# Linear attention into a gated feed-forward block: two quotients moved a group later, two chain operands in PSUM, the last first product moved ahead, low parts of the weights over 14 steps

## The chip, the cores and the metric

The kernel runs on one core of one Trainium2 chip. The metric is the device time of one execution in microseconds. The kernel before was timed three times, with a median of 1181.67 us. One more execution was taken by the hardware profiler; its own time and its span (first to last instruction) are in the table below.

Engines are named as the profile names them: PE (matrix products), PEld (its weight loads), DVE (VectorE), ACT (ScalarE), POOL (GpSimd), SP (the engine that issues most DMAs).

## The reference, cut to what matters

```
def _attn_ref(q, k, v, w_phi):                      # q, k, v: 8 x 8 x 576 x 64, w_phi: 64 x 128
    def phi(x):
        proj = einsum('bhsd,df->bhsf', x, w_phi)
        proj = proj - max(abs(proj), axis=-1)
        return concatenate([exp(proj), exp(-proj)], axis=-1)
    q_p, k_p = phi(q), phi(k)
    kv = einsum('bhsf,bhsd->bhfd', k_p, v)
    z = sum(k_p, axis=2)
    num = einsum('bhsf,bhfd->bhsd', q_p, kv)
    den = einsum('bhsf,bhf->bhs', q_p, z)[..., None] + 1e-06
    return num / den

def _moe_ref(x, w_in, w_out):                       # x: 4608 x 512, w_in: 512 x 2048, w_out: 2048 x 512
    h = x @ w_in
    g = h - tanh(h)
    return g @ w_out
```

The attention output, laid out as 4608 rows of 512, is the x of the second function. The weights w_in and w_out arrive as float64.

## The kernel before, in words

The work has two stages.

**First stage (attention).** A unit is one pair of heads of one batch entry; there are 32 units, and `period(i)` (line 399) runs five units at once, each one phase behind the next. The order of this stage is written out by hand (`tc.manual_schedule()`). A unit ends with a division. `denom_copy` puts the denominators in a tile `dd`, `den_recip_load` (line 346) brings them with a DMA into a narrow tile `dn`, `den_recip` (line 352) adds 1e-6 and inverts on DVE (`rn`, lines 357 and 358), sends the result to memory (`rr`) and back, broadcast, with two DMAs (`rb`, line 362). `den_mul` (line 365) multiplies numerator `d` by `rb` on POOL (line 367), and `x_store` writes the quotient to the array `xs`. The calls for the last units stand after the loop, at lines 490 to 496, outside the hand-written order.

**Second stage (feed-forward).** Tokens go in 12 groups of 384, the hidden width in 16 slices of 128, so there are 192 steps (g, f). `stage1` makes one slice of h: 12 products of 128 x 384 into the PSUM tile `ph` (line 516; three buffers), because each factor is split into a high part and a low part and three of the four cross products are kept, over four blocks of 128. Then comes a chain that forms h - tanh(h): ACT makes y = h squared (L523), `s1` (L525), `s2` (L527), `th` = tanh (L529) and a mask `mk` (L531; one buffer), and DVE makes five instructions of them:

```
            nc.vector.scalar_tensor_tensor(s1, s1, PC1, y, ALU.add, ALU.mult)        # L532
            nc.vector.scalar_tensor_tensor(s2, s2, PC2, s1, ALU.add, ALU.mult)       # L533
            nc.vector.scalar_tensor_tensor(gs, s2, PA, h, ALU.mult, ALU.mult)        # L535, gs = s2
            nc.vector.tensor_tensor(th, h, th, ALU.subtract)                         # L536
            nc.vector.copy_predicated(gs, mk.bitcast(U32), th)                       # L537
```

y, s1, s2, th and mk are in SBUF (two buffers each, `mk` one), h is in PSUM. `split_g` splits the result: ACT casts it to the high part `gh` (L543), POOL subtracts to get the low part `gl` (L544). `stage2` adds this slice's contribution to the three output tiles `po` of the group: six products of 128 x 512 with `gh` (L550, L551), then three with `gl` (L553). After 16 slices `store` copies the three tiles out of PSUM (ACT the second, DVE the other two) and writes them.

`stage1` of a step is followed by `stage2` of two steps before, so PE alternates between the two, and the chain has the time between to run. The split of the weights themselves (`split_w`, line 83) into `whi`/`who` and `wli`/`wlo` is done in the first stage for slices 0 to 6; slices 7 to 15 (18 tiles) are split in the first group's steps, by a rule on the step number at line 590: the cast of a `w_in` tile on ACT (L90), of a `w_out` tile on DVE (L92), and the low part of either on POOL (L96). The first group also splits the x of the second group (`x_split`: ACT L114, DVE L115).

Here no order is written by hand: a scheduler orders each engine's instructions, except that those wrapped in `pin` (casts, splits, low parts) keep their place in the program. Every engine runs its own instructions strictly in the order in which they stand; a buffer that is reused makes its writer wait for the last reader.

Of the kernel before, what the change touches and what calls it, by code (L numbers as in the profile page):

```python
# [8 lines left out]
F32 = mybir.dt.float32  # L9
F32R = mybir.dt.float32r  # L10
U32 = mybir.dt.uint32
# [8 lines left out]
P = 128  # L20
# [12 lines left out]
def tile_linear_attention_moe(  # L33
# [22 lines left out]
    G = 3  # L56
# [64 lines left out]
    with ExitStack() as c1:  # L121
# [230 lines left out]
        def den_recip(u, pin=lambda ins: ins):  # L352
            dn = u.dn
            rr = dr.tile([2, S], F32, tag="rr", name=f"rr{u.i}")
            w = 2 * S // P
            rn = tail.tile([P, w], F32, tag="rn", name=f"rn{u.i}")
            pin(nc.vector.tensor_scalar_add(rn, dn, 1e-6))
            nc.vector.reciprocal(rn, rn)
            nc.sync.dma_start(rr.rearrange("a s -> (a s)").rearrange("(p c) -> p c", c=w), rn)
            rb = tail.tile([P, S], F32, tag="rb", name=f"rb{u.i}", bufs=2)  # L360
            for e in range(2):
                nc.sync.dma_start(rb[e * D : (e + 1) * D, :], rr[e : e + 1, :].broadcast_to([D, S]))
            u.rb = rb

        def den_mul(u, pin=lambda ins: ins):
            x = u.rb
            pin(nc.gpsimd.tensor_tensor(x, u.d, x, ALU.mult))
# [123 lines left out]
        den_mul(units[-3])  # L491
        x_store(units[-3])
        den_recip_load(units[-1])
        den_recip(units[-2])
        den_mul(units[-2])
        x_store(units[-2])

    with ExitStack() as c2:  # L500
        xp.append(c2.enter_context(tc.tile_pool(name="xp", bufs=1, reuse_waits="tile")))
        wp.append(c2.enter_context(tc.tile_pool(name="wp", bufs=1, reuse_waits="tile")))
        gp = c2.enter_context(tc.tile_pool(name="gp", bufs=2, reuse_waits="tile"))
        gm = c2.enter_context(tc.tile_pool(name="gm", bufs=3, reuse_waits="tile"))
        ps_h = c2.enter_context(tc.tile_pool(name="ps_h", bufs=3, reuse_waits="tile", space=PSUM))
        ps_o = c2.enter_context(tc.tile_pool(name="ps_o", bufs=5, reuse_waits="tile", space=PSUM))

        def stage1(g, f, xh, xl):
            n = G
            N = n * P  # L510
            ph = ps_h.tile([P, 512], F32, tag="h", name=f"ph{g}_{f}")
            h = ph[:, 0:N]
            i = 0
            for c in range(NCT):
                for wt, x in ((wi[f][0], xh), (wi[f][0], xl), (wi[f][1], xh)):
                    nc.tensor.matmul(h, wt[:, c * P : (c + 1) * P], x[:, c, 0:N], start=(i == 0), stop=(i == 3 * NCT - 1))  # L516
                    i += 1

            def tmp(tag, dt=F32, pool=gp, **kw):
                return pool.tile([P, G * P], dt, tag=tag, name=f"{tag}{g}_{f}", **kw)[:, 0:N]  # L520

            y = tmp("y")
            nc.scalar.activation(y, h, AF.Square)  # L523
            s1 = tmp("s1")
            nc.scalar.activation(s1, y, AF.Square, bias=bias_t[:, 0:1])  # L525
            s2 = tmp("s2")
            nc.scalar.activation(s2, y, AF.Square, bias=bias_t[:, 1:2])  # L527
            th = tmp("th")
            nc.scalar.activation(th, h, AF.Tanh)  # L529
            mk = tmp("mk", bufs=1)  # L530
            nc.scalar.activation(mk, y, AF.Relu, bias=bias_t[:, 2:3])  # L531
            nc.vector.scalar_tensor_tensor(s1, s1, PC1, y, ALU.add, ALU.mult)  # L532
            nc.vector.scalar_tensor_tensor(s2, s2, PC2, s1, ALU.add, ALU.mult)  # L533
            gs = s2
            nc.vector.scalar_tensor_tensor(gs, s2, PA, h, ALU.mult, ALU.mult)  # L535
            nc.vector.tensor_tensor(th, h, th, ALU.subtract)  # L536
            nc.vector.copy_predicated(gs, mk.bitcast(U32), th)  # L537
            return gs

        def split_g(g, f, gs, n):  # L540
            gh = gm.tile([P, G * P], F32R, tag="gh", name=f"gh{g}_{f}")[:, 0 : n * P]
            gl = gm.tile([P, G * P], F32R, tag="gl", name=f"gl{g}_{f}")[:, 0 : n * P]
            pin(nc.scalar.copy(gh, gs))  # L543
            pin(nc.gpsimd.tensor_tensor(gl, gs, f32(gh), ALU.subtract))  # L544
            return gh, gl

        def stage2(po, f, gh, gl, n):
            for t in range(n):
                a = gh[:, t * P : (t + 1) * P]
                nc.tensor.matmul(po[t], a, wo[f][0], start=(f == 0), stop=False)  # L550
                nc.tensor.matmul(po[t], a, wo[f][1], start=False, stop=False)  # L551
            for t in range(n):
                nc.tensor.matmul(po[t], gl[:, t * P : (t + 1) * P], wo[f][0], start=False, stop=(f == NF - 1))  # L553

        def store(t, po, n):
            for i in range(n):
                o = gp.tile([P, DM], F32, tag="o", name=f"o{t + i}", bufs=3)
                if i == 1:
                    nc.scalar.copy(o, po[i])
                else:  # L560
                    nc.vector.tensor_copy(o, po[i])
                nc.sync.dma_start(out[(t + i) * P : (t + i + 1) * P, :], o)

        NG = NT // G
        steps = [(g, f) for g in range(NG) for f in range(NF)]
        late = list(range(2 * AHEAD, 2 * NF))
        NL = len(late)
        po, gs, gg = {}, {}, {}
        for i in range(len(steps) + 2):
            if i < len(steps):  # L570
                g, f = steps[i]
                if f == 0:
                    po[g] = [ps_o.tile([P, DM], F32, tag="o", name=f"po{g}_{t}") for t in range(G)]
                gs[i] = stage1(g, f, *xt[g][:2])
                if g + 1 < NG:
                    if f == 0:
                        xt[g + 1] = x_tiles(g + 1)
                    if f % 3 == 0 and f < 3 * NCT:
                        x_load(g + 1, xt[g + 1], f // 3)
                    if f % 3 == 2 and f < 3 * NCT:  # L580
                        x_split(xt[g + 1], f // 3, pin)
            if 1 <= i <= len(steps):
                g, f = steps[i - 1]
                gg[i - 1] = split_g(g, f, gs.pop(i - 1), G)
            if i == 1:
                den_recip(units[-1], pin)
            if i == 2:
                den_mul(units[-1], pin)
                x_store(units[-1])
            while late and late[0] <= 2 * AHEAD + i * NL // (NF - 1):  # L590
                split_w(late.pop(0), pin)()
            if i >= 2:
                g, f = steps[i - 2]
                stage2(po[g], f, *gg.pop(i - 2), G)
                if f == NF - 1:
                    store(g * G, po.pop(g), G)
# [55 lines left out]
```

## Time and profile before

| | |
|---|---|
| median of 3 runs (lowest, highest) | 1181.67 us (1179.06, 1183.47) |
| the profiled execution: time, span | 1179.44 us, 1177.6 us |
| granted PE clock, mean over the span | 0.998 |
| busy share of PE, PEld, DVE, ACT, POOL | 98%, 81%, 77%, 68%, 35% |
| first product of the second stage | 356.01 us |
| longest groups of the chain that ended last | PE ph L516 33%, PE po L553, L550 and L551 11% each |

PE is busy nearly all the time, so what another engine does shows in the time only where PE has to wait for it. Such places are read from the list of PE's waits and from the timeline; in the timeline a row gives the start, the duration, the engine, the line, the instruction, the tiles as output<-input, and in brackets the idle time of the engine before the row with what ended it.

### The profile page before, as it was taken

The page shows a single profiled execution, that of the slowest core. Times are in us where ns is not written, and L with a number is a line of the kernel's source. Part 1 is how long each engine was busy: PE and PEld are TensorE (multiplying, and loading weights), DVE is VectorE, ACT ScalarE, POOL GpSimd, SP SyncE. Part 2 cuts the span into 40 slices and gives each one's busy share as a digit, 9 for nine tenths or more (in the row PEclk, how much of TensorE's full clock was granted, in tenths as well). Part 3 has the DMA queues.
Part 4 walks back from the last instruction along what each step waited for, and adds up shares of the span by engine and source line. Part 5 has one row for each costly group of instructions (what it writes and reads, how often), then busy time and mean ns, then how long its engine had stood idle before and what let it go on. Part 6 is the DMA issues. An engine that isn't in the chain of part 4 may idle for free.

```text
span 1177.6 us, 21218 instructions
## 1 busy us (share of the span) xinstructions
PE 1157.2 (98%) x7840; PEld 950.1 (81%) x7840; DVE 907.6 (77%) x1464; ACT 806.0 (68%) x1748; POOL 412.6 (35%) x404
## 2 busy tenths in 40 slices
PE   8999999999998999999999999999999999999998
PEld 6666666666656889999999999999999999999996
DVE  6999998989877977777777767777777767777665
ACT  4777776666666767676676667676666767666665
POOL 2566664455435652222222222222222222222222
PEclk9999999999999999999999999999999999999999
DMA  5565565566551000010000001000000001000000
GB/s 165 178 194 190 180 206 183 189 189 209 182 177 61 14 19 30 14 41 15 34 14 34 21 8 41 14 34 21 34 14 35 15 13 41 14 28 1 28 1 28
DMA packets 51177, 85.64 MB, mean 73 GB/s; under 512 B 13312, under 2 KB 28160, under 8 KB 51072
## 3 DMA queue, kind: packets, MB, share of 16 engines
q1 hardware_dynamic: 50912, 84.20, 22.2%
q8 instruction: 62, 1.02, 0.3%
q14 instruction: 43, 0.35, 0.1%
q10 hardware_dynamic: 160, 0.07, 0.0%
HBM read 65.08 MB, written 19.02 MB: 71 GB/s over the span
## 4 chain that ended last, share of the span: by engine, by line
PE 91%; DVE 3%; POOL 2%; DMA 2%; ACT 1%; issue 1%; DVEq 0%; SPq 0%; POOLq 0%; ACTq 0%
PE ph L516 33%; PE po L553 11%; PE po L550 11%; PE po L551 11%; PE pp L214 7%; PE pc L267 6%; PE po L314 5%; PE ptt L236 3%; PE pd L329 3%; PE pk L285 2%; PE ptk L301 1%; DMA rb<-rr 1%; PE ptr L242 1%; DMA dn<-dd 1%; DVE s L537 0%
## 5 line engine op out<-in xcount | busy, mean ns | idle before, releaser
L544 POOL TENSOR_TENSOR gl<-s,gh 128x384 fp32r<-128x384 f32 x192 | 197.9, 1031 | 569.1 <-ACT gh L543 562.8
L516 PE MATMUL ph<-xh,wli 128*128 128x384 f32 x768 | 261.0, 340 | 1.3 <-POOL wli L96 1.3
L516 PE MATMUL ph<-xl,whi 128*128 128x384 f32 x768 | 260.2, 339 | 0.0
L516 PE MATMUL ph<-xh,whi 128*128 128x384 f32 x768 | 259.6, 338 | 0.3 <-DVE th L536 0.3
L523 ACT ACTIVATE y<-ph 128x384 f32<-128x384 f32 x192 | 94.5, 492 | 238.6 <-PE ph L516 238.6
L532 DVE SCALAR_TENSOR_TENSOR s<-s,y 128x384 f32<-128x384 f32 x192 | 107.8, 561 | 168.3 <-ACT s L525 168.2
L550 PE MATMUL po<-who,gh 128*128 128x512 f32 x576 | 227.1, 394 | 1.6 <-ACT gh L543 1.6
L551 PE MATMUL po<-wlo,gh 128*128 128x512 f32 x576 | 226.1, 393 | 0.0
L553 PE MATMUL po<-who,gl 128*128 128x512 f32 x576 | 164.8, 395 | 5.3 <-POOL gl L544 5.3
L537 DVE COPY_PREDICATED s<-mk,th 128x384 f32<-128x384 uint32 x192 | 140.3, 731 | 20.8 <-DVE th L536 1.4
L516 PEld LDWEIGHTS ph<-xh,whi 128*128 128x128 f32 x768 | 146.2, 190 | 9.0 <-DVE th L536 0.6
L516 PEld LDWEIGHTS ph<-xl,whi 128*128 128x128 f32 x768 | 144.6, 188 | 8.2
L516 PEld LDWEIGHTS ph<-xh,wli 128*128 128x128 f32 x768 | 144.9, 189 | 2.0 <-POOL wli L96 1.9
L553 PEld LDWEIGHTS po<-who,gl 128*128 128x128 f32 x576 | 107.9, 188 | 30.8 <-POOL gl L544 6.9
L533 DVE SCALAR_TENSOR_TENSOR s<-s,s 128x384 f32<-128x384 f32 x192 | 115.0, 599 | 20.1 <-ACT mk L531 0.9
L550 PEld LDWEIGHTS po<-who,gh 128*128 128x128 f32 x576 | 109.1, 189 | 20.7 <-ACT gh L543 3.4
L551 PEld LDWEIGHTS po<-wlo,gh 128*128 128x128 f32 x576 | 108.0, 187 | 16.8
L527 ACT ACTIVATE s<-y,bias_t 128x384 f32<-128x384 f32 x192 | 118.0, 615 | 4.9 <-POOL gl L544 4.7
L531 ACT ACTIVATE mk<-y,bias_t 128x384 f32<-128x384 f32 x192 | 117.9, 614 | 2.9 <-DVE s L537 2.9
L525 ACT ACTIVATE s<-y,bias_t 128x384 f32<-128x384 f32 x192 | 118.5, 617 | 0.0
L535 DVE SCALAR_TENSOR_TENSOR s<-s,ph 128x384 f32<-128x384 f32 x192 | 106.2, 553 | 6.3
L214 PEld LDWEIGHTS pp<-wph,qk 64*128 64x128 f32 x1152 | 73.4, 188 | 44.2 <-PE po L314 15.9
(75 smaller groups left out, 1707.8 us busy)
## 6 DMA issues: line engine op xcount, KB each, us to landing
qk<-in_qkT SPq DMA_DIRECT2D x31, 576.0 KB, 4.9
v<-in_v SPq DMA_DIRECT2D x32, 320.0 KB, 4.0
rb<-rr SPq DMA_DIRECT2D x64, 144.0 KB, 3.0
xs<-rb SPq DMA_DIRECT2D x32, 288.0 KB, 3.7
x<-xs SPq DMA_DIRECT2D x48, 192.0 KB, 2.3
out<-o SPq DMA_DIRECT2D x36, 256.0 KB, 2.1
rawi<-in_moe_w_in SPq DMA_DIRECT2D x16, 512.0 KB, 3.9
rawo<-in_moe_w_out SPq DMA_DIRECT2D x16, 512.0 KB, 6.3
```

Source lines behind the costliest of these rows:

```text
L214: nc.tensor.matmul(pp[e][:, a * F : (a + 1) * F], u.qk[hs, j * P : (j + 1) * P], wph[hs, :], start=True, stop=True)
L516: nc.tensor.matmul(h, wt[:, c * P : (c + 1) * P], x[:, c, 0:N], start=(i == 0), stop=(i == 3 * NCT - 1))
L525: nc.scalar.activation(s1, y, AF.Square, bias=bias_t[:, 0:1])
L527: nc.scalar.activation(s2, y, AF.Square, bias=bias_t[:, 1:2])
L531: nc.scalar.activation(mk, y, AF.Relu, bias=bias_t[:, 2:3])
L532: nc.vector.scalar_tensor_tensor(s1, s1, PC1, y, ALU.add, ALU.mult)
L533: nc.vector.scalar_tensor_tensor(s2, s2, PC2, s1, ALU.add, ALU.mult)
L537: nc.vector.copy_predicated(gs, mk.bitcast(U32), th)
L544: pin(nc.gpsimd.tensor_tensor(gl, gs, f32(gh), ALU.subtract))
L550: nc.tensor.matmul(po[t], a, wo[f][0], start=(f == 0), stop=False)
L551: nc.tensor.matmul(po[t], a, wo[f][1], start=False, stop=False)
L553: nc.tensor.matmul(po[t], gl[:, t * P : (t + 1) * P], wo[f][0], start=False, stop=(f == NF - 1))
```

## The change

Five edits, all in what follows the first stage:

1. The quotients of units 30 and 31 (`units[-2]`, `units[-1]`): `den_recip`, `den_mul` and `x_store` leave the end of the first stage and the steps 1 and 2; they now stand at steps 20 and 23 (unit 30) and 22 and 25 (unit 31), in the second group. The loads of `dn` stay where they were.
2. In the first group alone, `s2` and the difference h - th are kept in two PSUM tiles `ex0` and `ex1` (one buffer each, shared by the 16 steps; they take two of the five `po` buffers, which the first group leaves free), and `gs` is then `s1`. So L533 becomes `s1 <- ex0, s1` and L537 `s1 <- mk, ex1`, each with one operand in PSUM; the buffer that POOL's L544 holds is that of `s1` and no longer that of `s2`.
3. `stage1` of the last step is issued right after that of the step before it.
4. The rule for the split of the late weights divides by `NF - 2` = 14 in place of 15.
5. In the last group's `store`, ACT copies two tiles and DVE one, in place of one and two.

```diff
@@ after the loop over period(i)
         den_mul(units[-3])
         x_store(units[-3])
         den_recip_load(units[-1])
-        den_recip(units[-2])
-        den_mul(units[-2])
-        x_store(units[-2])
@@ pools of the second stage
         ps_o = c2.enter_context(tc.tile_pool(name="ps_o", bufs=5, reuse_waits="tile", space=PSUM))
+        ex = [ps_o.tile([P, DM], F32, tag="o", name=f"ex{a}")[:, 0 : G * P] for a in range(2)]
@@ stage1
-            s2 = tmp("s2")
+            s2 = tmp("s2") if g else ex[0]
             nc.scalar.activation(s2, y, AF.Square, bias=bias_t[:, 1:2])
...
             nc.vector.scalar_tensor_tensor(s1, s1, PC1, y, ALU.add, ALU.mult)
-            nc.vector.scalar_tensor_tensor(s2, s2, PC2, s1, ALU.add, ALU.mult)
-            gs = s2
-            nc.vector.scalar_tensor_tensor(gs, s2, PA, h, ALU.mult, ALU.mult)
-            nc.vector.tensor_tensor(th, h, th, ALU.subtract)
-            nc.vector.copy_predicated(gs, mk.bitcast(U32), th)
+            gs = s2 if g else s1
+            nc.vector.scalar_tensor_tensor(gs, s2, PC2, s1, ALU.add, ALU.mult)
+            nc.vector.scalar_tensor_tensor(gs, gs, PA, h, ALU.mult, ALU.mult)
+            hh = th if g else ex[1]
+            nc.vector.tensor_tensor(hh, h, th, ALU.subtract)
+            nc.vector.copy_predicated(gs, mk.bitcast(U32), hh)
             return gs
@@ store
-                if i == 1:
+                if (i == 1) == (t + n < NT):
                     nc.scalar.copy(o, po[i])
                 else:
                     nc.vector.tensor_copy(o, po[i])
@@ the loop over the steps
-                gs[i] = stage1(g, f, *xt[g][:2])
+                if i < len(steps) - 1:
+                    gs[i] = stage1(g, f, *xt[g][:2])
+                if i == len(steps) - 2:
+                    gs[i + 1] = stage1(g, f + 1, *xt[g][:2])
...
-            if i == 1:
-                den_recip(units[-1], pin)
-            if i == 2:
-                den_mul(units[-1], pin)
-                x_store(units[-1])
-            while late and late[0] <= 2 * AHEAD + i * NL // (NF - 1):
+            for n in (2, 1):
+                if i == NF + 8 - 2 * n:
+                    den_recip(units[-n], pin)
+                if i == NF + 11 - 2 * n:
+                    den_mul(units[-n], pin)
+                    x_store(units[-n])
+            while late and late[0] <= 2 * AHEAD + i * NL // (NF - 2):
                 split_w(late.pop(0), pin)()
```

Since a scheduler sets the order, three places show what the edits move. In the names, the first number of `gl0_3` or `ph11_14` is the group and the second the slice; the last number of every name is a running count.

POOL at the start of the second stage, before:

```order
L186 COPY mark_113<-wi15_4707 128x1
L367 TENSOR_TENSOR rb30_4764<-d30_4629,rb30_4764 128x576
L96 TENSOR_TENSOR wli7_4830<-wi7_2470,whi7_4829 128x512
L544 TENSOR_TENSOR gl0_0_4862<-s20_0_4814,gh0_0_4861 128x384
L96 TENSOR_TENSOR wlo7_4874<-wo7_2611,who7_4873 128x512
L544 TENSOR_TENSOR gl0_1_4908<-s20_1_4850,gh0_1_4907 128x384
L367 TENSOR_TENSOR rb31_4870<-d31_4731,rb31_4870 128x576
L96 TENSOR_TENSOR wli8_4914<-wi8_2752,whi8_4913 128x512
L544 TENSOR_TENSOR gl0_2_4957<-s20_2_4894,gh0_2_4956 128x384
```

POOL at the same place, changed:

```order
L186 COPY mark_113<-wi15_4707 128x1
L96 TENSOR_TENSOR wli7_4821<-wi7_2470,whi7_4820 128x512
L546 TENSOR_TENSOR gl0_0_4852<-s10_0_4804,gh0_0_4851 128x384
L96 TENSOR_TENSOR wlo7_4856<-wo7_2611,who7_4855 128x512
L546 TENSOR_TENSOR gl0_1_4889<-s10_1_4839,gh0_1_4888 128x384
L96 TENSOR_TENSOR wli8_4893<-wi8_2752,whi8_4892 128x512
L546 TENSOR_TENSOR gl0_2_4935<-s10_2_4874,gh0_2_4934 128x384
```

The two quotients `rb30` and `rb31` are gone from between the low parts; they now stand behind `gl1_6` and `gl1_8`.

ACT at the end of the program (`s111_15` is s1 of group 11, slice 15; `s211_15` is s2), before:

```order
L531 ACTIVATE mk11_14_12998<-y11_14_12990,bias_t_65 128x384
L543 CAST gh11_13_13005<-s211_13_12953 128x384
L523 ACTIVATE y11_15_13031<-ph11_15_13018 128x384
L529 ACTIVATE th11_15_13037<-ph11_15_13018 128x384
L525 ACTIVATE s111_15_13033<-y11_15_13031,bias_t_65 128x384
L527 ACTIVATE s211_15_13035<-y11_15_13031,bias_t_65 128x384
L531 ACTIVATE mk11_15_13039<-y11_15_13031,bias_t_65 128x384
L543 CAST gh11_14_13046<-s211_14_12994 128x384
L543 CAST gh11_15_13059<-s211_15_13035 128x384
L559 COPY o34_13084<-po11_1_12392 128x512
```

ACT at the same place, changed:

```order
L532 ACTIVATE mk11_14_12984<-y11_14_12976,bias_t_65 128x384
L524 ACTIVATE y11_15_13004<-ph11_15_12991 128x384
L530 ACTIVATE th11_15_13010<-ph11_15_12991 128x384
L526 ACTIVATE s111_15_13006<-y11_15_13004,bias_t_65 128x384
L532 ACTIVATE mk11_15_13012<-y11_15_13004,bias_t_65 128x384
L545 CAST gh11_13_13019<-s211_13_12939 128x384
L545 CAST gh11_14_13032<-s211_14_12980 128x384
L528 ACTIVATE s211_15_13008<-y11_15_13004,bias_t_65 128x384
L545 CAST gh11_15_13045<-s211_15_13008 128x384
L561 COPY o33_13067<-po11_0_12377 128x512
L561 COPY o35_13073<-po11_2_12379 128x512
```

The cast `gh11_13` stood right behind `mk11_14`; now four instructions of the last slice, `mk11_15` among them, stand ahead of it, and `s211_15` has slipped behind `gh11_14`.

DVE at the same place, before:

```order
L536 TENSOR_TENSOR th11_14_12996<-ph11_14_12977,th11_14_12996 128x384
L537 COPY_PREDICATED s211_14_12994<-mk11_14_12998,th11_14_12996 128x384
L532 SCALAR_TENSOR_TENSOR s111_15_13033<-s111_15_13033,y11_15_13031 128x384
L533 SCALAR_TENSOR_TENSOR s211_15_13035<-s211_15_13035,s111_15_13033 128x384
L535 SCALAR_TENSOR_TENSOR s211_15_13035<-s211_15_13035,ph11_15_13018 128x384
```

DVE at the same place, changed:

```order
L538 TENSOR_TENSOR th11_14_12982<-ph11_14_12963,th11_14_12982 128x384
L533 SCALAR_TENSOR_TENSOR s111_15_13006<-s111_15_13006,y11_15_13004 128x384
L539 COPY_PREDICATED s211_14_12980<-mk11_14_12984,th11_14_12982 128x384
L535 SCALAR_TENSOR_TENSOR s211_15_13008<-s211_15_13008,s111_15_13006 128x384
L536 SCALAR_TENSOR_TENSOR s211_15_13008<-s211_15_13008,ph11_15_12991 128x384
```

The first chain instruction of slice 15 now stands ahead of the last one of slice 14. On PE, the 12 products into `ph11_15` moved ahead of the nine of `stage2` of slice 12.

## The prediction

> **What bounds the kernel now.** I read the page first, then PE's waits, the timeline round them, and DVE's groups by form in two stretches.
>
> ```profile
> span 1177.6 us, 21218 instructions
> PE 1157.2 (98%) x7840; PEld 950.1 (81%) x7840; DVE 907.6 (77%) x1464; ACT 806.0 (68%) x1748; POOL 412.6 (35%) x404
> ```
>
> ```profile
> 356.00:423.00 67.00, 60.99 (x301) 52.87 (x297) 60.79 (x92) 48.97 (x105) 40.63 (x33) 1.00 0.11 35
> 498.00:565.00 67.00, 67.00 (x338) 60.77 (x337) 48.38 (x87) 46.71 (x102) 16.29 (x16) 1.00 0.08 24
> ```
>
> The second fence gives the busy time of PE, PEld, DVE, ACT and POOL in two stretches of 67 us, the first group and a later one. In the later one PE is never idle; in the first it is 6 us short, while DVE is busy for 61 of 67 us and POOL for 41 in place of 16. So there is something to win in the first group and almost nowhere else. PE's waits, second stage and first together (total, times, longest):
>
> ```profile
> PE po L553 <- POOL gl L544: 5.3, 4, 3.0
> PE po L550 <- ACT gh L543: 1.6, 2, 0.8
> PE ph L516 <- POOL wli L96: 1.3, 1, 1.3
> PE ph L516 <- DVE th L536: 0.3, 1, 0.3
> ```
>
> All of these but one of 0.8 lie in the first group (the other is in the last step). What the group loses is more than its waits. The timeline of PE shows the first product of the stage, the first of the second group, and one regular step:
>
> ```profile
> 356.01 0.44 PE L516 MATMUL ph<-xh,whi 128*128 128x384 f32 x1
> 430.75 0.34 PE L516 MATMUL ph<-xh,whi 128*128 128x384 f32 x1
> ...
> 1161.34 0.40 PE L550 MATMUL po<-who,gh 128*128 128x512 f32 x1
> 1163.41 0.34 PE L516 MATMUL ph<-xh,whi 128*128 128x384 f32 x1
> 1165.52 0.40 PE L550 MATMUL po<-who,gh 128*128 128x512 f32 x1
> ```
>
> A `stage1` takes 1165.52 - 1163.41 = 2.11 us, a `stage2` 1163.41 - 1161.34 = 2.07. Up to 430.75 PE has done 16 of the first and 14 of the second: 33.8 + 29.0 = 62.7 us. It took 74.74. The first group loses 12.0 us: 7.7 in waits (the rows above without the 0.8), and 4.3 in slow restarts and in a stretch at half clock, which the windows of PE alone show (busy time, count, granted clock):
>
> ```profile
> 364.67:368.09 3.42, 1.70 (x7) 1.00 0.21 84
> 422.70:426.11 3.41, 1.54 (x6) 1.00 0.00 0
> 426.11:429.52 3.41, 3.24 (x10) 0.50 0.02 5
> ```
>
> After a window in which PE was busy for only 1.54 of 3.41 us, the clock was 0.50 for the next 3.4 us, which costs about 3.41 / 2 = 1.7 us. The wait for `wli` (slice 15) lies just there.
>
> **The quotients (edit 1).** POOL, with rows of the others round it:
>
> ```profile
> 361.39 0.62 ACT L90 CAST whi<-wi 128x512 fp32r<-128x512 f32 x1
> 364.18 0.52 ACT L543 CAST gh<-s 128x384 fp32r<-128x384 f32 x1
> ...
> 365.05 1.44 POOL L367 TENSOR_TENSOR rb<-d,rb 128x576 f32<-128x576 f32 x1 [8.49 <-DMA rb<-rr]
> 366.44 1.59 POOL L96 TENSOR_TENSOR wli<-wi,whi 128x512 fp32r<-128x512 f32 x1
> 367.99 1.38 POOL L544 TENSOR_TENSOR gl<-s,gh 128x384 fp32r<-128x384 f32 x1
> 368.44 0.20 DVE L358 RECIPROCAL rn<-rn 128x9 f32<-128x9 f32 x1
> 369.42 0.96 PE L553 MATMUL po<-who,gl 128*128 128x512 f32 x3 [3.01 <-POOL gl L544]
> ...
> 375.03 1.46 POOL L367 TENSOR_TENSOR rb<-d,rb 128x576 f32<-128x576 f32 x1 [2.60 <-DMA rb<-rr]
> 379.24 0.97 PE L553 MATMUL po<-who,gl 128*128 128x512 f32 x3 [1.49 <-POOL gl L544]
> ```
>
> POOL stands 8.49 us at the head of its queue for the DMA of unit 30 while `whi7` is ready at 362.0; PE's longest wait (3.01 us) is for the `gl` at 367.99. Without it `wli7` runs from 362.05 to 363.4 and the first `gl` follows `gh` from 364.75 to 365.8; PE, which starts its six `gh` products at 364.75 too, at 2.07 / 9 = 0.23 us each, is ready for it at 366.2, so the wait goes. The second quotient (2.60 + 1.46 us) goes from in front of the third `gl`, and the wait of 1.49 us with it. What is late next: `s1` of step 2 goes into the buffer that this `gl` reads, so it starts at 365.85; `s2`, `mk`, `xh` and `gh` follow at 0.5 us each (as 1163.30 and 1163.81 below), `gh1` is there at 368.4, and PE, seven products of `stage1` behind its first `stage2`, wants it at 364.75 + 2.07 + 7 x 0.18 = 368.1. I leave 0.3 us for that, 0.3 for the start of the first `stage2`, and 0.45 for the wait on L536 with its restart, which nothing removes: 1.05 us.
>
> In the second group the moved work is hidden. POOL needs 16.3 us of 67 there, about 1.0 of each 4.18 us step, so two products of 1.45 us fit into the idle 3.1; if one blocks DVE, DVE's slack (67 - 48.4 over 16 steps, 1.2 us a step) takes it. Of the DMAs, `rr` and the two `rb` go through SP's queue three steps (12.5 us) ahead of the product; before, from `rn` to the product it was about 6.5 us for unit 31 (368.44 to 375.03). They stand behind a load of x for the fourth group and hold up the next such loads, which are read a group later. If that cover were gone, POOL would again hold a `gl`, for at most the 8.5 us seen above; I cost it at nothing.
>
> **Operands in PSUM (edit 2).** DVE's groups, mean ns behind the busy time, first in the crowded part of the first group (380 to 430), then in a quiet stretch (600 to 650):
>
> ```profile
> L537 DVE COPY_PREDICATED s<-mk,th 128x384 f32<-128x384 uint32 x11 | 12.8, 1160 | 1.1
> L533 DVE SCALAR_TENSOR_TENSOR s<-s,s 128x384 f32<-128x384 f32 x11 | 12.3, 1119 | 1.3 <-ACT s L527 0.3
> L535 DVE SCALAR_TENSOR_TENSOR s<-s,ph 128x384 f32<-128x384 f32 x11 | 6.1, 555 | 0.4
> ...
> L533 DVE SCALAR_TENSOR_TENSOR s<-s,s 128x384 f32<-128x384 f32 x12 | 6.7, 558 | 1.1
> L535 DVE SCALAR_TENSOR_TENSOR s<-s,ph 128x384 f32<-128x384 f32 x12 | 6.6, 553 | 0.4
> ```
>
> Both inputs of L533 and L537 are in SBUF, and where POOL works much they take twice as long; L535, with one input in PSUM, takes 555 ns in the one stretch and 553 in the other. L533 loses 0.56 us a step and L537, against its unhindered 0.6, as much. That 1.1 us is what keeps DVE from having slack in this group (60.8 of 67 us). No row has L533 or L537 with a PSUM input, DVE writing PSUM (L536 now) or ACT writing it (L527 now). By L535 the first two cost 0.55 to 0.6; a write may cost a little more or less than into SBUF. From below, no gain: 1.1 us a step stays; from above, all of it goes. I take all of it, L535 being the nearest row, and leave 0.95 us of the group's 12.0 for the instructions that still have two SBUF inputs (L532, the splits of x) and the `who` casts. The Trainium skill, SBUF — State Buffer, section "Who interferes with whom", has a rule for it: a VectorE instruction with two SBUF inputs contends with a GpSimd one that reads SBUF, one with at most one SBUF input does not. By that rule L533 and L537 are free of POOL, and L532 is not; the two stretches agree with it.
>
> The single buffer `ex0` adds a wait of L527 for the L533 before; `mk`, one buffer too, already waits for the later L537, and only half a microsecond later in ACT's queue, so nothing is added. `ex0` and `ex1` hold no `po` up: the second group's tiles are first written behind the last chain's `gh`.
>
> **Low parts over 14 steps (edit 4).** The cast `whi15` comes one step (4.18 us) sooner, ahead of `y14`. PE's order is now all of `ph15` ahead of `stage2` of slice 13, so the tile is wanted some 1 us sooner than before. Before it was 1.3 us late; now it is 4.2 - 1.0 - 1.3 = about 1.9 us early, less what POOL is behind. That wait and the half clock behind it go (3 us of the 12.0). The price is POOL with two weight tiles in three of the steps: 2 x 1.4 + 1.0 = 3.8 of 4.18 us, still inside.
>
> So the first group's 12.0 us fall to 1.05 + 0.95 = 2.0: **10.0 us gained**.
>
> **The last step (edits 3 and 5).** From the timeline of the end, before:
>
> ```profile
> 1163.30 0.61 ACT L531 ACTIVATE mk<-y,bias_t 128x384 f32<-128x384 f32 x1
> 1163.81 0.51 ACT L543 CAST gh<-s 128x384 fp32r<-128x384 f32 x1
> 1164.67 0.55 DVE L536 TENSOR_TENSOR th<-ph,th 128x384 f32<-128x384 f32 x1
> 1165.32 0.61 DVE L537 COPY_PREDICATED s<-mk,th 128x384 f32<-128x384 uint32 x1
> ...
> 1168.55 0.50 PE L550 MATMUL po<-who,gh 128*128 128x512 f32 x1 [0.79 <-ACT gh L543]
> 1168.63 1.02 POOL L544 TENSOR_TENSOR gl<-s,gh 128x384 fp32r<-128x384 f32 x1 [3.16 <-ACT gh L543]
> ...
> 1170.14 0.51 ACT L543 CAST gh<-s 128x384 fp32r<-128x384 f32 x1 [1.65 <-DVE s L537]
> 1170.74 0.47 PE L550 MATMUL po<-who,gh 128*128 128x512 f32 x1
> ...
> 1172.20 0.85 PE L553 MATMUL po<-who,gl 128*128 128x512 f32 x3
> ```
>
> The order that results is worse than the old one. ACT now has y15, tanh, `s1` and `mk15` between `mk14` and the cast `gh13`. On the old clock: `ph15` is ready at 1161.34 + 2.11 = 1163.45, y15 takes the place of `gh13` at 1163.81, `s1` ends at 1165.2. DVE runs L532 of slice 15 ahead of L537 of slice 14, which then ends at 1166.3 in place of 1165.93. `mk15` has one buffer and waits for that; `gh13` is done 1.0 us later, at 1167.35, in place of 1164.32. PE wants it at 1163.45 + 2.07 = 1165.52: **a new wait of about 1.85 us**. `gl13` ends at 1168.5, and only then may `s2` of slice 15 be written; 0.6 us for it, 2.3 for four DVE instructions, 0.55 for the cast: `gh15` at 1172.05. PE, from 1167.4, is through two `stage2` with a slow restart at 1171.65, waits 0.4, and needs 1172.20 + 0.85 - 1170.74 = 2.31 us: end at 1174.4 in place of 1173.05, 1.35 later. Two copies on ACT in place of DVE give back 0.1. So **1.25 us lost**; bounds are 0 (the scheduled order turns out no later than the old) and 1.9 (nothing of the new wait is made good by the 0.79 that goes).
>
> Sum: 10.0 - 1.25 = 8.75 us less. The profiled execution took 1179.44, its span and 1.84 around it, and lies 2.23 below the median; from it the sum gives 1170.7, from the median 1181.67 it gives 1172.9, which I predict.
>
> **Rivals.** (a) *The new wait at the end cools PE.* A 1.85 us wait leaves about 1.7 busy in a 3.41 us window; 1.54 was followed by half clock, 1.70 (364.67) was not. If it happens, 1.7 us more: 1174.6. The Trainium skill, TensorE: Matmul & The Clock Gate, "What's actually happening", ties half rate to an idle window of about 3.4 us, free-running; by that no wait here cools PE and the time is 1172.9, but the row at 426.11 came after a window that was 45% busy, so the row goes first.
>
> (b) *The blocking only moves.* L532, the `who` casts and the x splits meet POOL now, DVE stays at 4.2 us or more a step, and the waits behind 380 remain. Of the 7.7 us 0.3 + 3.0 + 1.5 lie ahead of 380 and 2.9 behind it; with restarts and some of the half clock 4 us stay there, 6 of the 12.0 in all. The tail is as above: 6.0 - 1.25 = 4.75 less, 1176.9. For it: after L537 the next DVE instruction no longer starts when POOL has just ended. Against it: at most one of them a step meets a long POOL instruction, where two did.
>
> (c) *Slower: the PSUM forms are dear.* L533, L536 and L537 work on PSUM for 16 steps. DVE needs about 3.3 us of a 4.18 us step when unhindered (48.4 / 16, and 0.3 for the casts). The gain is eaten when the group loses 10.75 again, 9.7 / 16 = 0.6 a step, with DVE at 4.8: 0.5 us more on each of the three, near twice their time. At 0.6 more each it is 0.9 x 16 + 1.05 = 15.5 lost, 3.5 + 1.25 slower: 1186.4. L535 and L536, which read PSUM at 0.55, speak against it.
>
> (d) *The tail does not get worse*: 1171.6.
>
> **How the numbers follow.** The forecast has 0.60 (its own range 1171 to 1175: 1 us either way in the first group, 0.6 in the tail, 0.5 for the median), (a) 0.13, (b) 0.16, (c) 0.04, (d) 0.07. A change of 0.5%, 5.9 us, is what a measurement of this kernel can tell. Faster than 1175.8 are the forecast, (a), (d) and a little of (b): 0.81; within it the rest of (b) and some of (c): 0.15; slower 0.04. The range reaches past (d) and to (b), with the runs' own scatter of 2 us: 1169.0 to 1177.2.
>
> **What would show it.** Right: no wait of PE for `gl` above 0.5 us up to 430 and none for `wli`; no window at 0.50 there; L533 and L537 near 0.6 us in the first group; the second group's first product at 420 to 422; a wait of PE for ACT's cast of 1.5 to 2 us some 9 us ahead of the end. Wrong: L532 or `who` at twice its time with PE waiting on; L536 well above 0.55; a half-clock window in the tail.

## The result, and the profile after

The changed kernel takes 1170.3 us (median of 4 runs, 1169.28 to 1173.59); the kernel before 1180.99 (4 runs, the three of its table further up and one more, 1179.06 to 1183.47). The ratio is 0.9924, with a 95% interval of 0.9903 to 0.9944: 0.8% faster. The profiled execution took 1170.24 us in place of 1179.44, 9.20 less. The lines of the second stage's functions that are named below have moved down by one or two: `ph` is L517 now, `s1` L526, the second square L528, `mk` L532, DVE's chain L533, L535, L536, L538 and L539 (for 532, 533, 535, 536, 537), `gh` L545, `gl` L546, the products of `stage2` L552, L553 and L555.

The page's span and first part, and the same two stretches of 67 us as before (PE, PEld, DVE, ACT and POOL busy, granted clock, DMA share, GB/s):

```profile
span 1168.4 us, 21231 instructions
PE 1154.4 (99%) x7840; PEld 949.5 (81%) x7840; DVE 896.1 (77%) x1463; ACT 805.1 (69%) x1749; POOL 409.7 (35%) x404
```

```profile
356.00:423.00 67.00, 66.56 (x337) 59.99 (x334) 56.76 (x97) 52.49 (x114) 40.26 (x35) 1.00 0.06 17
498.00:565.00 67.00, 67.00 (x338) 60.77 (x337) 48.38 (x87) 46.69 (x102) 16.30 (x16) 1.00 0.07 24
```

In the first of these stretches, which is the first group and now also the start of the second, PE is busy for 66.56 us where it was 60.99, and DVE for 56.76 where it was 60.79, although PE now gets through 337 products there and not 301. The later stretch is as before to 0.02 us. That the second group loses nothing by the quotients that it takes in shows in the ledger below (805.05 us with edit 1 alone, 805.04 before). PE's waits in the second stage (total, times, longest), and PE's timeline at the start of the first group, at its one wait, at its second `stage2`, and at the start of the second group:

```profile
PE po L552 <- ACT gh L545: 2.1, 2, 1.7
PE ph L517 <- DVE ex L538: 0.4, 1, 0.4
```

```profile
356.05 0.44 PE L517 MATMUL ph<-xh,whi 128*128 128x384 f32 x1
363.05 0.45 PE L517 MATMUL ph<-xh,whi 128*128 128x384 f32 x1 [0.43 <-DVE ex L538]
368.50 0.50 PE L552 MATMUL po<-who,gh 128*128 128x512 f32 x1
420.19 0.34 PE L517 MATMUL ph<-xh,whi 128*128 128x384 f32 x1
```

No wait for `gl` or `wli` is left. The second group starts 420.19 - 356.05 = 64.14 us after the first, and 62.74 of them (16 x 2.11 + 14 x 2.07) are products: the first group loses 1.40 us where it lost 12.00. Nearly all of that is lost ahead of 368.50: up to there PE has done 52 products of `stage1` and nine of `stage2`, 11.21 us of work, in 12.45 us; for the other 51.53 us of work it takes 51.69. The other wait, for `gh`, is new and lies in the last step; ACT and PE there:

```profile
1154.00 0.63 ACT L526 ACTIVATE s<-y,bias_t 128x384 f32<-128x384 f32 x1
1155.75 0.61 ACT L532 ACTIVATE mk<-y,bias_t 128x384 f32<-128x384 f32 x1 [1.12 <-DVE s L539]
1156.27 0.91 ACT L545 CAST gh<-s 128x384 fp32r<-128x384 f32 x2
1156.81 0.50 PE L552 MATMUL po<-who,gh 128*128 128x512 f32 x1 [1.68 <-ACT gh L545]
1157.94 0.62 ACT L528 ACTIVATE s<-y,bias_t 128x384 f32<-128x384 f32 x1 [0.77 <-POOL gl L546]
1161.07 0.51 ACT L545 CAST gh<-s 128x384 fp32r<-128x384 f32 x1 [2.51 <-DVE s L539]
1161.63 0.50 PE L552 MATMUL po<-who,gh 128*128 128x512 f32 x1 [0.40 <-ACT gh L545]
1163.12 0.85 PE L555 MATMUL po<-who,gl 128*128 128x512 f32 x3
```

ACT stands 1.12 us in front of `mk15`, whose one buffer L539 of slice 14 still reads; the cast `gh13` queues behind it and PE waits 1.68 us for that cast. `s2` of slice 15 then waits for `gl13`, and PE 0.40 us for the last cast.

### One ledger for all kernels

Every kernel below ran the same 16 + 14 steps of PE up to the second group's first product, so each profile can be cut in three: when the second stage starts, what the first group loses (time from the first product to the second group's first, less 62.74 us), and the rest of the stage (from PE's last product's end, less the start and the loss). The last three columns come from PE's timeline in the one profiled execution of each kernel; all times are in us.

| kernel | median of runs | ratio to before, 95% | 2nd stage starts | group 1 loses | rest of the stage |
|---|---|---|---|---|---|
| before | 1180.83 (23 runs) | | 356.01 | 12.00 | 805.04 |
| changed | 1170.30 | 0.9924, 0.9903 to 0.9944 | 356.05 | 1.40 | 806.52 |
| edit 1 alone | 1175.00 | 0.9964, 0.9943 to 0.9985 | 355.13 | 6.89 | 805.05 |
| edit 2 alone | 1177.23 | 0.9976, 0.9966 to 0.9986 | 358.03 | 8.10 | 805.05 |
| edit 4 alone | 1176.70 | 0.9967, 0.9953 to 0.9981 | 356.77 | 8.86 | 805.05 |
| changed, edit 1 undone | 1176.53 | 0.9970, 0.9957 to 0.9983 | 356.39 | 5.84 | 806.52 |
| changed, operands in SBUF | 1176.24 | 0.9964, 0.9949 to 0.9979 | 360.22 | 4.35 | 806.52 |
| changed, only `ex0` in PSUM | 1173.31 | 0.9938, 0.9920 to 0.9955 | 359.74 | 1.42 | 806.53 |
| changed, only `ex1` in PSUM | 1174.55 | 0.9952, 0.9936 to 0.9967 | 357.18 | 3.89 | 806.53 |
| changed, edit 4 undone | 1174.59 | 0.9954, 0.9937 to 0.9971 | 357.89 | 3.83 | 806.52 |
| changed, edit 3 undone | 1170.39 | 0.9915, 0.9901 to 0.9930 | 357.99 | 1.06 | 805.05 |
| changed, last products behind the split | 1168.48 | 0.9900, 0.9886 to 0.9914 | 357.32 | 1.73 | 803.89 |

The rest of the stage has only three values, and which one is decided by edit 3 and its place alone. The start scatters by 5 us, and the order of the work does not set it: in all twelve profiles PE, DVE, ACT and POOL run the same instructions in the same order up to 2 us ahead of the second stage. Part of it is the clock: in the first stage the kernel with its operands in SBUF had two windows at 0.50, the one with `ex0` alone and the one with edit 3 undone had one each, and the others none. This scatter is noise in the medians, which the ledger takes out. Each ratio is to the runs of the kernel before that were made in the same batch; the medians of those lie between 1179.94 and 1180.99 us, and batches ran on different chips, so that medians of different batches cannot be compared to better than about 1 us.

### The profile page after: what moved, and what is told of

Its sections match the earlier page's. It is cut to its first block, busy times and chain, and to the rows that moved or that the text cites. A ratio compares the mean times of both kernels' runs of the same rounds, so it can differ in the third digit from the quotient of the medians.

```text
span 1168.4 us, 21231 instructions
## 1 busy us (share of the span) xinstructions
PE 1154.4 (99%) x7840; PEld 949.5 (81%) x7840; DVE 896.1 (77%) x1463; ACT 805.1 (69%) x1749; POOL 409.7 (35%) x404
## 4 chain that ended last, share of the span: by engine, by line
PE 94%; DMA 2%; DVE 1%; ACT 1%; POOL 1%; issue 0%; SPq 0%; ACTq 0%; POOLq 0%; DVEq 0%
PE ph L517 34%; PE po L552 11%; PE po L555 11%; PE po L553 11%; PE pp L214 7%; PE pc L267 6%; PE po L314 5%; PE ptt L236 3%; PE pd L329 3%; PE pk L285 2%; PE ptk L301 1%; DMA rb<-rr 1%; PE ptr L242 1%; DMA rr<-rn 0%; DMA dn<-dd 0%
## 5 line engine op out<-in xcount | busy, mean ns | idle before, releaser
L546 POOL TENSOR_TENSOR gl<-s,gh 128x384 fp32r<-128x384 f32 x192 | 195.5, 1018 | 567.6 <-ACT gh L545 563.8
L517 PE MATMUL ph<-xh,wli 128*128 128x384 f32 x768 | 260.1, 339 | 0.0
L517 PE MATMUL ph<-xl,whi 128*128 128x384 f32 x768 | 259.7, 338 | 0.0
L517 PE MATMUL ph<-xh,whi 128*128 128x384 f32 x768 | 259.1, 337 | 0.4 <-DVE ex L538 0.4
L533 DVE SCALAR_TENSOR_TENSOR s<-s,y 128x384 f32<-128x384 f32 x192 | 110.1, 573 | 168.6 <-ACT s L526 168.5
L552 PE MATMUL po<-who,gh 128*128 128x512 f32 x576 | 227.0, 394 | 2.1 <-ACT gh L545 2.1
L553 PE MATMUL po<-wlo,gh 128*128 128x512 f32 x576 | 226.1, 392 | 0.0
L555 PE MATMUL po<-who,gl 128*128 128x512 f32 x576 | 164.4, 394 | 0.0
L517 PEld LDWEIGHTS ph<-xh,whi 128*128 128x128 f32 x768 | 145.8, 190 | 9.1 <-DVE ex L538 0.7
L517 PEld LDWEIGHTS ph<-xl,whi 128*128 128x128 f32 x768 | 144.2, 188 | 8.1
L517 PEld LDWEIGHTS ph<-xh,wli 128*128 128x128 f32 x768 | 144.3, 188 | 0.0
L539 DVE COPY_PREDICATED s<-mk,th 128x384 f32<-128x384 uint32 x176 | 123.3, 701 | 18.3 <-DVE th L538 0.5
L555 PEld LDWEIGHTS po<-who,gl 128*128 128x128 f32 x576 | 108.2, 188 | 24.1
L552 PEld LDWEIGHTS po<-who,gh 128*128 128x128 f32 x576 | 109.0, 189 | 21.0 <-ACT gh L545 3.6
L553 PEld LDWEIGHTS po<-wlo,gh 128*128 128x128 f32 x576 | 108.0, 187 | 17.0
L526 ACT ACTIVATE s<-y,bias_t 128x384 f32<-128x384 f32 x192 | 118.5, 617 | 0.3 <-POOL gl L546 0.3
L532 ACT ACTIVATE mk<-y,bias_t 128x384 f32<-128x384 f32 x192 | 117.6, 612 | 1.1 <-DVE s L539 1.1
L535 DVE SCALAR_TENSOR_TENSOR s<-s,s 128x384 f32<-128x384 f32 x176 | 98.4, 559 | 20.7 <-ACT s L528 2.9
L536 DVE SCALAR_TENSOR_TENSOR s<-s,ph 128x384 f32<-128x384 f32 x192 | 106.3, 553 | 6.3
L528 ACT ACTIVATE s<-y,bias_t 128x384 f32<-128x384 f32 x176 | 108.2, 615 | 0.8 <-POOL gl L546 0.8
```

What stands on the lines that cost most here:

```text
L536: nc.vector.scalar_tensor_tensor(gs, gs, PA, h, ALU.mult, ALU.mult)
L539: nc.vector.copy_predicated(gs, mk.bitcast(U32), hh)
```

## The experiments

**Each edit by itself.** Three kernels take the kernel before and add one edit. The first, edit 1:

```
-        den_recip(units[-2]); den_mul(units[-2]); x_store(units[-2])   # ahead of the second stage
...
-            if i == 1: den_recip(units[-1], pin)
-            if i == 2: den_mul(units[-1], pin); x_store(units[-1])
+            for n in (2, 1):
+                if i == NF + 8 - 2 * n: den_recip(units[-n], pin)
+                if i == NF + 11 - 2 * n: den_mul(units[-n], pin); x_store(units[-n])
```

> Edit 1 alone on the kernel before: the two quotients moved to the second group, all else as before. By the theory (two separate causes in the first group: POOL held up by the quotients, and DVE held up by POOL because L533 and L537 have both inputs in SBUF) the two waits for gl of 3.0 and 1.5 us go and the later ones stay: the first group loses 5 to 7 us in place of 12.0, L533 and L537 stay near 1.1 us between 380 and 430, 5 to 7 us less time (ratio 0.994 to 0.996). By the rival (the quotients made a backlog that caused the later waits too) the group loses 2 to 3 us, 9 to 10 us less time (0.992).

Measured: 1175.00 us, loss 6.89, so 5.1 us gained, as the theory said. PE's waits:

```profile
PE po L547 <- ACT gh L540: 2.2, 4, 0.8
PE ph L513 <- POOL wli L96: 1.3, 1, 1.3
PE po L550 <- POOL gl L541: 0.8, 2, 0.7
```

The two long waits for `gl` behind the quotients are gone, and no window of the group is at half clock; the wait for `wli15` is as long as before, though.

The second, edit 2 (`s2 = tmp("s2") if g else ex[0]`, `gs = s2 if g else s1`, `hh = th if g else ex[1]`, and the two tiles):

> Edit 2 alone on the kernel before: ex0 and ex1 in PSUM in the first group, all else as before. By the theory L533 and L537 fall to 0.6 us there, the waits behind 380, with the wait for the low part of slice 15 and its half clock, go or nearly so, and the two waits for gl behind the quotients stay: the group loses 5 to 7 us in place of 12.0, 5 to 7 us less time (0.994 to 0.996). By the rival (the operands' place does not matter, the quotients did it all) the group loses 11 to 12 us and the time is that of before (1.000).

Measured: 1177.23 us, loss 8.10, 3.9 gained, less than the 5 to 7 that the theory said. L535 and L539 are at 557 and 601 ns from 380 to 420 us, as it said, but PE still waits where the quotients and the last slice are; the wait for `wli` became shorter, 0.77 us in place of 1.3, and did not go:

```profile
371.05 1.56 PE L555 MATMUL po<-who,gl 128*128 128x512 f32 x3 [2.57 <-POOL gl L546]
423.53 0.50 PE L552 MATMUL po<-who,gh 128*128 128x512 f32 x1 [0.79 <-ACT gh L545]
425.85 0.44 PE L517 MATMUL ph<-xh,wli 128*128 128x384 f32 x1 [0.77 <-POOL wli L96]
```

The third, edit 4:

```
-            while late and late[0] <= 2 * AHEAD + i * NL // (NF - 1):
+            while late and late[0] <= 2 * AHEAD + i * NL // (NF - 2):
```

> Edit 4 alone on the kernel before: the late weights over 14 steps in place of 15, all else as before. By the theory the wait for the low part of slice 15 (1.3 us) and the half clock behind it (1.7 us) go, the waits for gl stay or grow a little since DVE is already the slow engine there: the group loses 9 to 10 us in place of 12.0, 2 to 3 us less time (0.998). By the rival (DVE and POOL are full, so the same work sooner only moves the wait) the group loses 11 to 13 us and the time is that of before.

Measured: 1176.70 us, loss 8.86, 3.1 gained, just above the 2 to 3 expected. The wait for `wli` is gone; the wait of 3.11 us for the first `gl` stays, and the clock behind it shows in PE's windows (busy, count, granted clock, DMA share, GB/s):

```profile
366.42:369.84 3.42, 0.97 (x5) 1.00 0.22 86
369.84:373.25 3.41, 2.75 (x8) 0.50 0.19 43
373.25:376.66 3.41, 3.41 (x10) 0.50 0.35 107
```

5.1, 3.9 and 3.1 make 12.1 where the three together gain 10.6: the edits take away nearly separate losses. Taking one out of the changed kernel asks the same from the other end.

**Edit 1 undone in the changed kernel** (the diff above, backwards).

> The changed kernel with edit 1 undone: the quotients of the last two units stand again at their old places, edits 2 to 4 stay. Edit 1 alone cut the first group's loss from 12.00 to 6.89 us, edits 2 and 4 alone by 3.9 and 3.1; the three together left 1.40. Theory A (the edits remove separate waits, so undoing one gives back what it gained alone): the loss is 1.4 + 5.1 = 6.5 us, with a wait for gl of over 2 us and a half-clock window behind it, and the time about 1175.5. Theory B (the chain with PSUM operands leaves VectorE enough slack to take the quotients in): the loss is 2 to 3 us, no half-clock window, the time about 1171.5.

Measured: 1176.53 us, loss 5.84. POOL at the head of its queue, and PE behind it:

```profile
365.67 1.43 POOL L367 TENSOR_TENSOR rb<-d,rb 128x576 f32<-128x576 f32 x1 [8.74 <-ACT y L527]
367.06 1.27 POOL L96 TENSOR_TENSOR wli<-wi,whi 128x512 fp32r<-128x512 f32 x1
368.28 1.18 POOL L549 TENSOR_TENSOR gl<-s,gh 128x384 fp32r<-128x384 f32 x1
369.51 1.16 PE L558 MATMUL po<-who,gl 128*128 128x512 f32 x3 [2.65 <-POOL gl L549]
```

POOL stands idle for 8.74 us again (the waiting instruction is the quotient; the releaser that the trace names here is another than before, and I rest nothing on it), and a half-clock window follows PE's wait: 2.65 + 1.7 is the 4.4 us that come back. Theory A is right for the first quotient. The second one, which cost a wait of 1.49 us before, costs none now, so for that one theory B holds.

**Edit 4 undone in the changed kernel** (`NF - 2` back to `NF - 1`).

> The changed kernel with edit 4 undone: the low parts of the weights are spread over 15 steps again, edits 1 to 3 stay. Theory A (the last slice's low part comes too late whatever else is done, as with edit 1 alone, where the wait for wli of 1.3 us was still there): a wait for wli of 1 to 1.5 us near 418, the loss 2.5 to 4.5 us, the time about 1172 to 1173. Theory B (the casts were late only because VectorE was): no wait for wli over 0.2 us, the loss about 1.4 us, the time 1170.3 as now.

Measured: 1174.59 us, loss 3.83, 2.4 more than with the edit. PE near the end of the group:

```profile
419.12 0.50 PE L552 MATMUL po<-who,gh 128*128 128x512 f32 x1 [0.79 <-ACT gh L545]
421.44 0.44 PE L517 MATMUL ph<-xh,wli 128*128 128x384 f32 x1 [0.79 <-POOL wli L96]
```

Theory A, with a shorter wait than it said and a second one beside it: a VectorE with slack does not bring the last low part in time, since it is issued too late. No clock window was lost.

**The operands.** The changed kernel with `ex0` and `ex1` in SBUF, one buffer each, so that the order and the waits between instructions stay:

```
-        ex = [ps_o.tile([P, DM], F32, tag="o", name=f"ex{a}")[:, 0 : G * P] for a in range(2)]
+        ex = [gp.tile([P, G * P], F32, tag=f"ex{a}", name=f"ex{a}", bufs=1)[:, 0 : G * P] for a in range(2)]
```

> The changed kernel with ex0 and ex1 in SBUF in place of PSUM, still one buffer each; every instruction stands where it stands in the changed kernel, and all the waits are the same. By the theory (the place of the operand is what counts) L535 and L539, the old L533 and L537, are back near 1.1 us in the first group, DVE needs 4.3 us a step again, and the group loses 4 to 6 us in place of 1.4: 3 to 5 us more than the changed kernel. By the rival (what counts is which buffer POOL holds, s1 in place of s2, and the shorter queue on POOL) the group loses 1.4 to 2 us and the time is that of the changed kernel.

Then only one of them in PSUM: `hh = th` for the kernel with `ex0` alone, `s2 = tmp("s2")` and `gs = s2` for the one with `ex1` alone.

> The changed kernel with ex0 alone in PSUM: L535 has an operand there, L539 has both in SBUF again (h - th goes back into th). By the theory of the place of the operand L535 is near 0.56 us and L539 near 1.1 us in the first group, DVE needs about 3.8 to 4.0 us of a step of 4.18, and the group loses 1.4 to 2.5 us: up to 1 us more than the changed kernel. By the rival (both are needed, since what is freed is taken by the other's wait) it loses 4 to 5 us, as with both in SBUF.

> The changed kernel with ex1 alone in PSUM: L539 has an operand there, L535 has both in SBUF, and the result is in s2 again, whose buffer POOL holds, as in the kernel before. By the theory L539 is near 0.6 us, L535 near 1.1 us, and the group loses 1.4 to 2.5 us. By the rival (both are needed) it loses 4 to 5 us; if it loses more than with ex0 alone, the buffer that POOL holds counts too.

DVE's groups from 380 to 420 us, both in SBUF:

```profile
L535 DVE SCALAR_TENSOR_TENSOR s<-ex,s 128x384 f32<-128x384 f32 x10 | 12.0, 1195 | 1.0
L539 DVE COPY_PREDICATED s<-mk,ex 128x384 f32<-128x384 uint32 x9 | 10.6, 1174 | 0.9
...
L533 DVE SCALAR_TENSOR_TENSOR s<-s,y 128x384 f32<-128x384 f32 x9 | 5.0, 552 | 0.0
```

`ex0` alone in PSUM:

```profile
L539 DVE COPY_PREDICATED s<-mk,th 128x384 f32<-128x384 uint32 x10 | 7.9, 794 | 1.0
L533 DVE SCALAR_TENSOR_TENSOR s<-s,y 128x384 f32<-128x384 f32 x10 | 6.6, 656 | 1.3 <-ACT s L526 1.2
...
L92 DVE CAST who<-wo 128x512 fp32r<-128x512 f32 x6 | 5.5, 913 | 0.0
L535 DVE SCALAR_TENSOR_TENSOR s<-ex,s 128x384 f32<-128x384 f32 x9 | 5.0, 557 | 0.9
```

`ex1` alone in PSUM:

```profile
L535 DVE SCALAR_TENSOR_TENSOR s<-s,s 128x384 f32<-128x384 f32 x10 | 12.3, 1233 | 1.0
L539 DVE COPY_PREDICATED s<-mk,ex 128x384 f32<-128x384 uint32 x10 | 6.0, 601 | 1.0
L533 DVE SCALAR_TENSOR_TENSOR s<-s,y 128x384 f32<-128x384 f32 x10 | 5.8, 582 | 0.5 <-ACT s L526 0.5
```

And both, the changed kernel:

```profile
L533 DVE SCALAR_TENSOR_TENSOR s<-s,y 128x384 f32<-128x384 f32 x10 | 8.6, 858 | 3.9 <-ACT s L526 3.8
L539 DVE COPY_PREDICATED s<-mk,ex 128x384 f32<-128x384 uint32 x10 | 6.0, 600 | 1.0
L538 DVE TENSOR_TENSOR ex<-ph,th 128x384 f32<-128x384 f32 x10 | 5.6, 559 | 0.0
...
L535 DVE SCALAR_TENSOR_TENSOR s<-ex,s 128x384 f32<-128x384 f32 x9 | 5.0, 558 | 0.9
L115 DVE TENSOR_TENSOR xl<-x,xh 128x384 fp32r<-128x384 f32 x3 | 3.6, 1199 | 0.0
```

With nothing else changed, L535 goes from 1195 to 558 ns and L539 from 1174 to 600 when one operand is in PSUM: this is what the Trainium skill, SBUF — State Buffer, "Who interferes with whom", says of a VectorE instruction with fewer than two SBUF inputs, and these runs agree. The rival of the first run, that the buffer POOL holds is what counts, put the loss at 1.4 to 2 us; it is 4.35. But the two kernels with one operand in PSUM do not do equally well. `ex0` alone gives a loss of 1.42 us, all that both give; `ex1` alone leaves 3.89 of the 4.35, where 1.4 to 2.5 were expected. The second of them differs in one thing more: its result is in `s2` again, the buffer that POOL's L546 reads. Between 356 and 420 us ACT waits for that buffer for 0.8 us (L528), and with `ex0` alone for 1.4 us for the one of `s1` (L526), so the wait for it does not look like the cause; but no run takes the two apart, and why `ex1` alone leaves so much stays open. The blocking does move on: with `ex0` alone to L539 (794), L533 (656) and the `who` casts (913, where with both in SBUF they take 415; they have one input alone, and why they are slowed no run here tells), in the changed kernel to L533 and the splits of x; the chain is blocked less all the same. Adding the five means of the chain with L536 and L538 at 0.55 each gives DVE 4.0 us a step with both in SBUF, 3.5 with `ex1`, and 3.1 both with `ex0` and with the two in PSUM. So `ex1` could have stayed in SBUF. By the medians (1173.31 against 1170.30) one would say otherwise, but in the profile of the kernel with `ex0` alone the second stage starts 3.7 us later, and up to there the two run the same instructions.

**The last products.** Edit 3 undone (`stage1` of the last slice back in its own step):

> The changed kernel with the last step's first product where it was before (edit 3 undone, edit 5 kept). By the theory (the order on ACT and DVE that edit 3 brings costs more at the end than it saves) PE's two waits for gh at the end, 1.68 and 0.40 us, become one of 0.8 us and the kernel is 1.2 to 1.5 us faster than the changed one. By the rival (the end is bound by the chain of the last slice, whatever the order) the end stays within 0.3 us of the changed kernel's.

and, in its place, `stage1` of the last slice issued in the step before, but behind that step's `split_g`:

```
             if 1 <= i <= len(steps):
                 g, f = steps[i - 1]
                 gg[i - 1] = split_g(g, f, gs.pop(i - 1), G)
+            if i == len(steps) - 2:
+                g, f = steps[i + 1]
+                gs[i + 1] = stage1(g, f, *xt[g][:2])
```

> The changed kernel with the last step's first product still a step sooner on PE, but written behind the split of the slice two before: ACT has the cast gh11_13 ahead of y11_15 again, and DVE the L539 of slice 14 ahead of the L533 of slice 15. By the theory neither wait at the end is left (gh11_13 1.2 us ahead of its use, gh11_14 0.6 us, gh11_15 0.1 to 0.3 us), the end is 2.2 to 2.5 us sooner than the changed kernel's and about 1 us sooner than with edit 3 undone. By the rival (mk11_15, with one buffer, holds gh11_14 up) a wait of 0.3 to 1 us for gh11_14 takes the place and the kernel is as fast as with edit 3 undone.

With edit 3 undone PE waits once at the end, as in the kernel before:

```profile
1159.60 0.50 PE L552 MATMUL po<-who,gh 128*128 128x512 f32 x1 [0.79 <-ACT gh L545]
```

Behind the split, `gh13` stands again right behind `mk14` on ACT and ahead of the last chain, and PE's last two casts' products start without a wait:

```profile
1154.85 0.51 ACT L545 CAST gh<-s 128x384 fp32r<-128x384 f32 x1
1155.25 0.50 ACT L524 ACTIVATE y<-ph 128x384 f32<-128x384 f32 x1
...
1158.63 0.39 PE L552 MATMUL po<-who,gh 128*128 128x512 f32 x1
1160.70 0.39 PE L552 MATMUL po<-who,gh 128*128 128x512 f32 x1
```

The rest of the stage is 805.05 us without edit 3, 806.52 with it, 803.89 with it behind the split. The traces take this apart. The kernel without edit 3 and the one behind the split run the same order on ACT, DVE and POOL and differ on PE alone: the earlier products gain 1.16 us. The one behind the split and the changed kernel run the same order on PE and differ in the last step on ACT and DVE: that costs 2.63. So edit 3 loses 1.47 us as it stands, by the order that it brings to ACT and DVE. The medians do not show it (1170.39 without edit 3, 1170.30 with it, where 1.2 to 1.5 less was expected): in the profile without edit 3 the second stage starts 1.94 us later. Behind the split the kernel is the fastest of all: 1168.48 us (1167.51 to 1169.13), 1.0% below the kernel before, and none of its four runs reaches the lowest of the changed kernel's (1169.28), though the intervals of the two ratios overlap.

## Why the prediction was right

Forecast 1172.9 us in a range of 1169.0 to 1177.2, measured 1170.3. Against the profiled execution the sum was -8.75 us and came out at -9.20: the start of the second stage +0.04, the first group -10.60, the rest of the stage +1.48, from PE's end to the end of the execution -0.12. Most of the 2.6 us between forecast and median is the anchor, which is scatter and no part of the mechanism. 0.84 is that 1181.67 was the median of 3 runs and 23 runs of the same kernel give 1180.83; 1.33 is that before's profiled execution lay 1.39 below its median and the changed kernel's only 0.06; 0.45 is the sum itself.

- *First group, 10.0 predicted, 10.6 measured.* The waits for `gl` (both), for `wli`, and the half clock are gone, and undoing edit 1 or edit 4 brings back the wait that it was said to remove (of the two for `gl`, the first). The term that was mis-sized is the 0.95 us left for instructions that still have two SBUF inputs and for the `who` casts: behind 368.50 only 0.16 are lost. The 1.05 for the start became 1.24, of which the wait on L538 is 0.43.
- *Rival (b), the blocking only moves.* Its premise came true: from 380 to 420 us L533 took 858 ns, where the same instruction (L532 then) took 547 before, and the splits of x 1199 in place of 548. Its price did not: DVE's chain still fell to about 3.1 us of a 4.18 us step, DVE is busy for 33.8 of those 40 us, and it now waits for ACT (3.9 us ahead of L533), not PE for it. The blocked instructions cost PE nothing here, since DVE had slack. Two inputs in SBUF are not enough to be slowed: L532 had them before too, and in that stretch it was not.
- *Operands, "I take all of it".* 558 and 600 ns against the 0.55 to 0.6 read from L535. A write into PSUM by DVE takes 559 ns (L538, 551 into SBUF), so rival (c) had no ground. That both operands were needed is what the prediction assumed and the runs did not bear out.
- *The quotients at nothing in the second group.* The later groups are unchanged and PE does not wait there; the cover that was named held.
- *Low parts.* 3 us was put on the wait and the clock window behind it; alone the edit gained 3.1, and 2.4 in company, where no clock window was at stake.
- *The last step, 1.25 lost.* Waits of 1.85 and 0.4 predicted, 1.68 and 0.40 measured; PE's end 1.35 later predicted, 1.48 measured; copies 0.1 back, 0.11 measured (4.51 us from PE's end to the end of the span before, 4.40 after). Undoing edit 3 shows, in the profiles, that the loss is its own. The new wait lies 11.6 us ahead of the end of the span, and not the 9 that were named.
- *Rival (a), the clock in the last step.* It did not happen in any of the profiles with edit 3, and by little; PE's window there, in the changed kernel:

```profile
1153.81:1157.22 3.41, 1.73 (x8) 1.00 0.01 2
```

## What to carry to other kernels

When several engines wait on each other in a crowded stretch, price each wait by itself and add: here three edits to one group gave 10.6 of the 12.1 us that they gave alone. Before moving a piece of work forward "so that it is ready sooner", follow each engine's queue: what it puts ahead of a cast that someone waits for can cost more than it brings (here 2.63 against 1.16 us), and a few lines further down the same move pays. Where VectorE and GpSimd share a stretch, one operand in PSUM can be enough; here it was the first of the two blocked instructions that had to be freed. Compare stage by stage when medians scatter by more than the edit.

## What the runs showed of the hardware

The granted clock drops after a window that is far from idle. In the second stage's profiles, windows of 3.41 us with PE busy for 0.77, 0.84, 0.97 and 1.54 us were followed by one at 0.50, those with 1.71, 1.72, 1.73, 1.76, 1.92 and 2.07 were not. In the kernel with edit 4 alone a window at half clock with 2.75 us busy was followed by a second one at half, while in the kernel before one with 3.24 us at half clock was followed by full: halved, these are 1.38 and 1.62, on the same two sides. So in this stage the bound lies near 1.6 of 3.41 us of full-speed work. The Trainium skill, TensorE: Matmul & The Clock Gate, "What's actually happening", speaks of an idle window; that is not what these rows show. Nor is busy time the whole of it: in the first stage, with other shapes of products, windows of 1.84 (changed, edit 3 undone), 2.09 (changed, only `ex0` in PSUM), 2.23 and 2.55 us (changed, operands in SBUF) were followed by half clock, while others of 2.14 and 2.23 us in the last two kernels were not. The highest of them, and the window behind it:

```profile
240.50:243.91 3.41, 2.55 (x37) 1.00 0.16 42
243.91:247.33 3.42, 3.42 (x23) 0.50 0.95 293
```

Why that is, no run here tells.
